# A linear-attention kernel with a gated state space layer: a new order of the opening, and other turns in two steps of its main loop

## The chip, the cores and the metric

One core of a Trainium2 chip runs the whole kernel. The metric is the device time of one execution in microseconds (us). Engines are named as in the profile: PE is TensorE's matrix multiplication and PEld its weight load, DVE is VectorE, ACT is ScalarE, POOL is GpSimd, SP is SyncE, which here only issues transfers.

## The reference

```python
def _attn_ref(q, k, v, alpha):               # each (4, 8, 768, 48)
    state = np.zeros((B, H, D, D))
    for t in range(S):
        state = alpha[:, :, t, :, None] * state + np.einsum('bhd,bhe->bhde', k[:, :, t], v[:, :, t])
        y[:, :, t] = np.einsum('bhd,bhde->bhe', q[:, :, t], state)
    return y

def _moe_ref(x, w_in, A_log, w_out):         # w_in (384, 1024), w_out (512, 384)
    proj = x @ w_in
    val, gate = proj[..., :D_inner], proj[..., D_inner:]
    a = np.exp(A_log)
    for t in range(S):
        h = a * h + val[:, t, :]
        ys[:, t, :] = h
    return (gate / (1 + np.exp(-gate)) * ys) @ w_out

# x is y as (4, 768, 8 * 48)
```

A recurrent attention with a decay for each element and step, in 4 batches of 8 heads, feeds a projection, a scan over time, a gate and a second projection. w_in, A_log and w_out arrive as float64.

## The kernel before, in words

`fast` cuts each batch's 768 steps into 3 groups of 256, 12 groups in all (0 to 11). A group has two chunks of 128 steps (c) and four of 64 (u). Heads 0 to 3 lie in partitions 0 to 63, heads 4 to 7 in 64 to 127 (i is 0 or 1).

**Attention of a group m.** alpha, q and k are turned, so that the steps lie along the free dimension. For groups 0 to 3 (alpha) and 0 to 2 (q, k) TensorE does it: `turned` writes a PSUM bank with 8 or 16 small products against the identity, or by transposes for a few named cases, and `copy_turned` copies it out. From then on VectorE transposes blocks of 32 (`turn`). VectorE runs two scans over a group, `scan_P` forward (running products of alpha, P) and `scan_V` backward (V), and multiplies: Zk is k times V, Zq is q times P. `scores` are products of Zk and Zq into two banks with tags s0, s1 (chunk 0) and two of the four shared banks "mm" (chunk 1). `masks` multiplies by a triangle on VectorE (A) and copies the rest on ACT; from group 3 on, half of the masking is done by POOL on AK. `values` multiplies with v into the banks y, `states` forms the states of the chunks, `add_up` or `add_banks` sums these (sum), `carried` adds what earlier states bring, and `join` copies the result out and moves it by transfers into xT, heads side by side. The main loop calls `first` (scores, masks), `second` (across values, states, sums on POOL) and `third` (carried, values, join).

**State space layer of a group n.** `project(n, cc)` for cc 0 to 3: 6 products of xT with w_in into a pair of "mm" banks, a scan on VectorE (hh), Silu on ACT (sg), a product sg times hh (f). The pairs of banks take turns, so a projection waits until the one before the last has been read by its scan and its Silu. `output(n)` multiplies f with w_out, 8 products of 384 columns, and stores.

**Order.** The schedule is written by hand: each engine runs its instructions in the order of the program's text, and waits for what they need. Step n of the main loop works on layer n and on attention m = n + 1. VectorE's work for groups 4 to 11 is a generator, `products`, of seven pieces (alpha turned, P, k turned, V, Zk, q turned, Zq); `go(count)` runs the next pieces. In steps 3 to 10 a step reads: second(m), go(4), project 0, go(1), project 1, go(1), project 2, go(1), project 3, third(m), first(m+1), output(n). In step 2 the order is first(3), go(1), project 0, second(3), go(2), and so on.

**Weights.** Both weight matrices come as 64-bit words and are made into 32-bit floats: ACT takes the low bits (`low`), VectorE the high ones, POOL adds. w_in is loaded in three units of columns: cc 0, cc 1, cc 2 and 3.

**Opening.** Transfers of alpha, q, k of group 0 go out in two halves, by SP (heads 0 to 3) and by ACT (heads 4 to 7). TensorE warms up on zeros (`keep_warm`), turns alpha, q, k of group 0, then alpha, k of group 1, and so on as attention of group 0 permits; all of q of group 1 is turned between its scores and its values. A small write of POOL into raw_a keeps the second set of loads back.

Of the kernel before, what the change touches and what calls it, by code (L numbers as in the profile page):

```python
# [9 lines left out]
FP32 = mybir.dt.float32  # L10
# [336 lines left out]
def fast(  # L347
# [41 lines left out]
    p2 = pool("p2", 2)  # L389
    ps_at = pool("ps_at", 1, space=PS)  # L390
# [56 lines left out]
    units = [range(0, 1), range(1, 2), range(2, 4)]  # L447
# [45 lines left out]
    def constants():  # L493
# [22 lines left out]
        nc.vector.memset(K0[:, :, :, D:], 0.0)  # L516
# [22 lines left out]
    def low(i):  # L539
        bits, w = bits_of(i)  # L540
        r = p2.tile([C, UW], I32, tag="wr", name="wr")
        lows[i] = r.rearrange("p (a n) -> p a n", a=w.shape[1])
        halves = lows[i].bitcast(U16).rearrange("p a (n two) -> p a n two", two=2)
        nc.scalar.activation(halves[:, :, :, 0], bits[:, :, :, 0], AF.Copy, scale=2.0 ** -29)

    def convert(i):
        if i not in lows:
            low(i)
        bits, w = bits_of(i)
        r = lows.pop(i)  # L550
        halves = r.bitcast(U16).rearrange("p a (n two) -> p a n two", two=2)
        quarters = bits.rearrange("p a n two -> p a (n two)").bitcast(U16).rearrange("p a (n four) -> p a n four", four=4)
        nc.vector.tensor_scalar(out=w.bitcast(U32), in0=bits[:, :, :, 1], scalar1=3, scalar2=0x3FFFFFFF,
                                op0=ALU.logical_shift_left, op1=ALU.bitwise_and)
        nc.vector.tensor_scalar(out=halves[:, :, :, 1], in0=quarters[:, :, :, 3], scalar1=0xC000, scalar2=None,  # L555
                                op0=ALU.bitwise_and)
        nc.gpsimd.tensor_tensor(out=w.bitcast(I32), in0=w.bitcast(I32), in1=r, op=ALU.add)  # L557
# [126 lines left out]
    def turned(m, name, js, t):  # L684
        raw = steps_of(name, m)
        tp = t[:, 0:len(js) * C].rearrange("p (j x) -> p j x", j=len(js))
        if (m, name) in ((1, "k"), (1, "q"), (3, "a")):
            for n, j in enumerate(js):
                nc.tensor.transpose(tp[:, n], raw[:, ds(ROW + j * D - 64, C)], ident)  # L689
                nc.tensor.transpose(tp[0:64, n], raw[:, ds(j * D, 64)], ident)  # L690
            return tp.rearrange("p j (c h) -> p h c j", h=4)
# [6 lines left out]
    def copy_turned(to, js, tp, engine=None):  # L698
        place = by_runs(to)[:, :, :, js.start:js.stop]
        if engine:  # L700
            return engine.tensor_copy(out=place, in_=tp)
        return nc.scalar.activation(place, tp, AF.Copy)

    def turn_over(m, name, to, tags=(None, None)):
        size = NJ // len(tags)
        copies = []
        for n, tag in enumerate(tags):
            js = range(size * n, size * (n + 1))
            copy = copy_turned(to, js, turned(m, name, js, bank(tag)), nc.vector if n % 2 and tag else None)
            if tag:  # L710
                for other in copies[(n + 1) % 2::2]:
# [3 lines left out]
    def alphas(m, tags=(None, None)):  # L715
        turn_over(m, "a", by_place(als[m % 2])[:, :, 1:GP], tags)
# [31 lines left out]
    def masks(m):  # L748
        sc = [[t[:, 0:4 * (L + D)].rearrange("p (h x) -> p h x", h=4) for t in pair] for pair in scs.pop(m)]
        mb = mask[:, None, :]  # L750
        if m < NG:
            for c in range(G):
# [162 lines left out]
    def project(n, cc, late=False):  # L915
# [10 lines left out]
        for vg, kk in order:  # L926
            nc.tensor.matmul((pv, pg)[vg], w_ins[cc][:, kk, vg, :], xT[:, kk, :],  # L927
                             start=(kk == 0), stop=(kk == NK - 1))
# [10 lines left out]
        sg = p2.tile([C, GC], FP32, tag="sg", name="sg")  # L939
# [43 lines left out]
    alphas(0, ("s0", "s1", "y1", "y0"))  # L983
    tq = straighten(0, "q")
    tk = straighten(0, "k")
    alphas(1)
    P = scan_P(0)
    V = scan_V(0, P, False)
    halves = [range(0, NJ // 2), range(NJ // 2, NJ)]
    parts = [turned(1, "k", js, bank()) for js in halves]  # L990
# [3 lines left out]
    scores(0)  # L994
    tk = plain("k")
    for js, part in zip(halves, parts):
        copy_turned(tk, js, part)
    low(0)
    parts = [turned(1, "q", js, bank()) for js in halves]
    convert(0)  # L1000
    nc.gpsimd.memset(raws["a"][0:1, 0:1], 0.0)
    load_steps("a", 2, [nc.sync])
    load_w(units[2], nc.sync)
    masks(0)
    low(1)
    first_values(True)
    st = states(0)
    convert(1)
    first_states(st)
    tq = plain("q")  # L1010
    for js, part in zip(halves, parts):
        copy_turned(tq, js, part)
    last = P[:, :, GC]
    nc.scalar.activation(ratio[:, 0], last, AF.Copy, scale=1.0 / FIRST_PRODUCT)
    nc.scalar.activation(lower[:, :, 0], last, AF.Copy)
    for name in "kqa":
        load_steps(name, 2 + (name == "a"), [nc.sync])
    load_v(1, nc.sync)
# [3 lines left out]
    first_carried((2, 3))  # L1022
    first_join()
    nc.scalar.activation(a_dec, a_log, AF.Exp)
# [25 lines left out]

    for n in range(N):
        m = n + 1
        if n == 0:
            V = scan_V(1, P)
            f0 = project(n, 0)
# [3 lines left out]
            f1 = project(n, 1)  # L1059
# [168 lines left out]
```

## Time and profile before

| | |
|---|---|
| three executions | 279.72 us median, 278.26 to 280.07 |
| the profiled execution | 279.43 us, of which the span from first to last instruction is 277.7 us |
| PE busy | 268.8 us (97%) |
| DVE busy | 218.3 us (79%) |
| POOL busy | 122.4 us (44%) |
| ACT busy | 108.6 us (39%) |
| granted TensorE clock | 1.000 over the span |
| first projection (L927) starts at | 23.39 us |
| last output products start at | 269.30 us |

The timeline gives for each engine the start, the length, the line, the tiles (out<-in) and the number of instructions of a run, and in brackets how long the engine stood idle before it and what ended that. The chain of waits goes back from the last instruction, at each step to what released it. A matmul on 32-bit floats appears as two records, a transpose as one.

### The profile page before, as it was taken

How to read it: one execution, taken by the hardware profiler on the slowest of the kernel's cores; microseconds unless marked ns; L12 is line 12 of the kernel's file. 1: busy time of each engine (PE TensorE's matmuls, PEld its weight loads, DVE VectorE, ACT ScalarE, POOL GpSimd, SP SyncE). 2: the span in 40 equal slices, each digit the busy share in tenths (PEclk: the TensorE clock that was granted, in tenths of full speed). 3: DMA queues.
4: the chain of work that ended last, by engine and by line, in shares of the span. 5: the costliest groups of instructions: out<-in, count | busy, mean ns of one | idle time of the engine just before them, and what ended most of it. 6: DMA issues, size and time to landing. Idle time of an engine off the chain costs nothing.

```text
span 277.7 us, 9598 instructions
## 1 busy us (share of the span) xinstructions
PE 268.8 (97%) x4056; PEld 217.0 (78%) x4056; DVE 218.3 (79%) x281; ACT 108.6 (39%) x244; POOL 122.4 (44%) x141
## 2 busy tenths in 40 slices
PE   7999999999989999899999999999999999999995
PEld 5988887876678688488688688688688688787874
DVE  7979998898798995995895995996995993079540
ACT  2577763461332532341542433433434425213111
POOL 8141223130068574563473584484384476435000
PEclk9999999999999999999999999999999999999999
DMA  6949993845919777487468587576687501201201
GB/s 196 295 140 309 296 262 78 205 88 139 267 48 238 149 199 182 103 214 163 103 181 199 114 205 164 130 197 155 152 186 159 144 0 27 77 1 33 71 5 59
DMA packets 51599, 41.18 MB, mean 148 GB/s; under 512 B 27360, under 2 KB 49536, under 8 KB 51552
## 3 DMA queue, kind: packets, MB, share of 16 engines
q1 hardware_dynamic: 48752, 37.50, 53.1%
q0 software_dynamic: 1408, 2.03, 2.8%
q10 hardware_dynamic: 1392, 0.99, 1.2%
q8 instruction: 33, 0.54, 0.9%
q14 instruction: 14, 0.11, 0.2%
HBM read 32.54 MB, written 4.72 MB: 134 GB/s over the span
## 4 chain that ended last, share of the span: by engine, by line
PE 92%; DVE 3%; DMA 1%; POOL 1%; issue 1%; ACT 1%; SPq 0%; DVEq 0%; ACTq 0%
PE mm L927 45%; PE mm L956 21%; PE y L791 4%; PE y L778 4%; PE mm L744 3%; PE s L744 3%; PE s L810 3%; PE mm L694 2%; PE mm L1189 2%; DMA raw_a<-in_alpha_dram 1%; POOL AK L762 1%; DVE P L630 1%; DVE V L649 1%; PE mm L689 1%; PE y L862 1%
## 5 line engine op out<-in xcount | busy, mean ns | idle before, releaser
L927 PE MATMUL mm<-xT,w_in 128*128 128x256 f32 x576 | 128.9, 382 | 0.6 <-ACT xT L884 0.6
L927 PEld LDWEIGHTS mm<-xT,w_in 128*128 128x128 f32 x576 | 108.1, 190 | 16.3 <-issue 0.8
L956 PE MATMUL mm<-w_out,f_last 128*128 128x384 f32 x160 | 54.1, 492 | 1.3 <-DVE A L759 1.3
L940 ACT ACTIVATE sg<-mm 128x256 f32<-128x256 f32 x48 | 18.4, 384 | 85.8 <-PE mm L927 80.3
L956 PEld LDWEIGHTS mm<-w_out,f_last 128*128 128x128 f32 x160 | 29.7, 190 | 21.1 <-issue 1.4
L830 POOL TENSOR_TENSOR sum<-sum,dS 128x192 f32<-128x192 f32 x30 | 33.2, 1108 | 27.3 <-PE mm L927 13.5
L942 POOL TENSOR_TENSOR f_last<-sg,hh 128x256 f32<-128x256 f32 x36 | 30.9, 862 | 30.6 <-ACT sg L940 23.1
L932 DVE TENSOR_TENSOR_SCAN hh<-a_dec,hh,mm 128x256 f32<-128x256 f32 x32 | 23.4, 732 | 15.4 <-PE mm L927 15.2
L630 DVE TENSOR_TENSOR_SCAN P<-al,lower 128x1028 f32<-128x1028 f32 x12 | 31.1, 2595 | 0.6
L649 DVE TENSOR_TENSOR_SCAN V<-al,ends 128x1028 f32<-128x1028 f32 x12 | 28.3, 2356 | 0.4
L907 POOL DMA_DIRECT2D xT<-yst x40 | 20.5, 517 | 13.1 <-ACT yst L904 11.8
L950 ACT ACTIVATE o_sb<-mm 128x384 f32<-128x384 f32 x22 | 10.8, 491 | 38.4 <-PE mm L956 38.4
L762 POOL TENSOR_TENSOR AK<-AK,mask 128x512 f32<-128x512 f32 x9 | 13.2, 1464 | 17.2 <-ACT AK L760 17.2
L759 DVE TENSOR_TENSOR A<-s,mask 128x256 f32<-128x256 f32 x9 | 3.8, 425 | 21.5 <-PE s L744 21.5
L557 POOL TENSOR_TENSOR w_in<-w_in,wr 128x768 int32<-128x768 int32 x4 | 7.3, 1826 | 26.0 <-DVE wr L555 17.0
L595 DVE STREAM_TRANSPOSE k<-raw_k 128x1024 f32<-128x1024 f32 x9 | 18.3, 2033 | 0.0
L595 DVE STREAM_TRANSPOSE q<-raw_q 128x1024 f32<-128x1024 f32 x9 | 18.2, 2022 | 0.0
L778 PEld LDWEIGHTS y<-AK,v 64*64 64x64 f32 x352 | 12.1, 134 | 6.4 <-issue 5.0
L595 DVE STREAM_TRANSPOSE al<-raw_a 128x1024 f32<-128x1024 f32 x8 | 16.3, 2041 | 0.1
L778 PE MATMUL y<-AK,v 64*64 64x64 f32 x352 | 14.5, 221 | 1.0 <-POOL AK L762 1.0
L791 PEld LDWEIGHTS y<-Zq,sum 48*64 48x64 f32 x656 | 11.8, 134 | 4.3 <-issue 4.1
L791 PE MATMUL y<-Zq,sum 48*64 48x64 f32 x656 | 14.4, 221 | 0.6 <-issue 0.6
(158 smaller groups left out, 392.2 us busy)
## 6 DMA issues: line engine op xcount, KB each, us to landing
v<-in_v_dram SPq DMA_DIRECT2D x22, 192.0 KB, 3.3
out_dram<-o_sb SPq DMA_DIRECT2D x22, 192.0 KB, 2.1
raw_k<-in_k_dram SPq DMA_DIRECT2D x18, 184.0 KB, 3.4
raw_q<-in_q_dram SPq DMA_DIRECT2D x18, 184.0 KB, 3.8
raw_k<-in_k_dram SPq DMA_DIRECT2D x18, 176.0 KB, 3.8
raw_q<-in_q_dram SPq DMA_DIRECT2D x18, 176.0 KB, 4.1
raw_a<-in_alpha_dram SPq DMA_DIRECT2D x16, 184.0 KB, 5.0
raw_a<-in_alpha_dram SPq DMA_DIRECT2D x16, 176.0 KB, 5.1
```

The costliest lines, as they stand in the source:

```text
L595: nc.vector.transpose(out=by_runs(to).rearrange("p h c j -> p h j c"), in_=raws[name][:, 0:4 * ROW].rearrange("p (h j d) -> p h j d", h=4, ...
L630: nc.vector.tensor_tensor_scan(out=P, data0=al[:, 0:4 * GP], data1=lower.rearrange("p h t -> p (h t)"), initial=0.0, op0=ALU.mult, op1=ALU ...
L649: nc.vector.tensor_tensor_scan(out=V[:, ::-1], data0=al[:, 1:4 * GP + 1][:, ::-1], data1=ends.rearrange("p h t -> p (h t)")[:, ::-1], init ...
L778: nc.tensor.matmul(ys[m][i][ds(64 * s, 64), e, ds(c * C + h * L, L)], v_sb[rows, c, 4 * i + p, :], As[i][rows, c, p, :], start=across and ...
L791: nc.tensor.matmul(ys[m][i][ds(64 * s, 64), e, ds(u * L, L)], Ss[j][rows, p, :], Zqs[m % 2][rows, u, p, D:], start=False, stop=True, skip_ ...
L830: nc.gpsimd.tensor_add(Ss[j][:, :, 0:D], Ss[j - 1][:, :, 0:D], part)
L907: engines[n % len(engines)].dma_start(out=xT[to, a], in_=st[rows, i, e])
L927: nc.tensor.matmul((pv, pg)[vg], w_ins[cc][:, kk, vg, :], xT[:, kk, :], start=(kk == 0), stop=(kk == NK - 1))
L932: nc.vector.tensor_tensor_scan(out=hh, data0=a_dec[:, cc:cc + 1].to_broadcast([C, GC]), data1=pv, initial=prev_h[cc][:, GC - 1:GC] if n % ...
L940: nc.scalar.activation(sg, pg, AF.Silu)
L942: f = lambda: engine.tensor_mul(fs[n][cc], sg, hh)
L956: nc.tensor.matmul(os[c], fs[n][cc][:, ds(c * C, C)], w_outs[cc // 2][:, cc % 2, :], start=(cc == 0), stop=(cc == NI - 1))
```

## The change

- `first_alphas` turns alpha of group 0 by products of 64x64, thirty-two in place of sixteen, into the same four banks by quarters, heads 4 to 7 first; ACT copies two banks and VectorE two, as before.
- `first_q` turns q of group 0 with heads 4 to 7 a few products ahead, and the last four of heads 0 to 3 by transposes. k of group 0 and alpha of group 1 are turned by transposes.
- Memsets of dS, of K0 and of the pads of sums leave VectorE; the pads are written by six copies on ACT.
- k and q of group 1 are turned and copied by halves: half of k ahead of the scores, half behind them, half of q then, and the last half behind the carried products of group 0. The masks of group 0 are called by chunks, the first unit's high bits between them. The second unit's bits are taken in two halves ahead of `first_states`.
- The write that keeps the second loads back is made by ACT, later. The upper half of w_in's columns is loaded as two units, the second behind k, q and alpha; its low bits are taken later (`low(3)`).
- In step 0 the third projection is cut in two, with values, states and sums of group 1 between. The products f of the first two projections move to step 1 (sg gets four buffers for that).
- In step 2 `second(3)` moves behind project 1. In step 3 `first(5)` moves behind output(3), and in step 4 `second(5)` moves behind project 1, with go(2) ahead of project 0 and go(2) behind it.

```diff
+    gates = pool("gates", 4)
...
-    units = [range(0, 1), range(1, 2), range(2, 4)]
+    units = [range(i, i + 1) for i in range(NI)]
...
-        for t in dS[0] + dS[1]:
-            nc.vector.memset(t[:, :, :, D:64], 0.0)
-        for t in sums:
-            nc.vector.memset(t[:, :, D:64], 0.0)
-        nc.vector.memset(K0[:, :, :, D:], 0.0)
...
+    turned_by_transpose = ((0, "k"), (1, "a"), (1, "k"), (1, "q"), (3, "a"))
...
+    def first_alphas():
+        raw, to = steps_of("a", 0), by_runs(by_place(als[0])[:, :, 1:GP])
+        tps = [[bank(tag)[:, 0:NJ // 2 * 64].rearrange("p (j x) -> p j x", x=64) for tag in tags]
+               for tags in (("s0", "s1"), ("y1", "y0"))]
+
+        def turn_quarter(j, i, r):
+            rows = ds(64 * r, 64)
+            nc.tensor.matmul(tps[j // 4][r][ds(64 * i, 64), j % 4], raw[rows, ds(i * ROW + j * D, 64)],
+                             ident[rows, rows], start=True, stop=True, skip_group_check=True)
+
+        for j in range(2):
+            for r in range(2):
+                turn_quarter(j, 1, r)
+        for j in range(NJ):
+            for r in range(2):
+                turn_quarter(j, 0, r)
+                if j + 2 < NJ:
+                    turn_quarter(j + 2, 1, 1 - r)
...
     keep_warm(3, 256)
-    alphas(0, ("s0", "s1", "y1", "y0"))
-    tq = straighten(0, "q")
+    first_alphas()
+    for t in sums:
+        nc.scalar.activation(t[:, :, D:64], wide_S[0][:, 0:4 * (64 - D)].rearrange("p (j d) -> p j d", j=4), AF.Copy)
+    tq = first_q()
     tk = straighten(0, "k")
     alphas(1)
     P = scan_P(0)
...
-    parts = [turned(1, "k", js, bank()) for js in halves]
+    part = turned(1, "k", halves[0], bank())
     for c in range(G):
         scaled_k(0, tk, V, c)
         scaled_q(0, tq, P, c)
...
+    copy_turned(tk, halves[0], part)
+    for c in range(G):
+        scores(0, (c,))
+    part = turned(1, "k", halves[1], bank())
+    masks(0, (0,))
     low(0)
+    high(0)
+    masks(0, (1,))
+    add_low(0)
+    copy_turned(tk, halves[1], part)
+    part = turned(1, "q", halves[0], bank())
+    first_values(True)
+    st = states(0)
+    for vg in range(2):
+        low(1, slice(vg, None, 2))
+        high(1, slice(vg, None, 2))
+    first_states(st)
+    add_low(1)
+    copy_turned(tq, halves[0], part)
+    nc.scalar.activation(raws["a"][0:1, 0:1], wide_S[1][0:1, D:D + 1], AF.Copy)
     load_steps("a", 2, [nc.sync])
     load_w(units[2], nc.sync)
...
+    load_w(units[3], nc.sync)
     load_v(1, nc.sync)
     P = scan_P(1)
     first_carried((1,))
     first_values(False)
     first_carried((2, 3))
+    part = turned(1, "q", halves[1], bank(), False)
     first_join()
+    copy_turned(tq, halves[1], part)
...
+    late = (1, 3)
...
-            f2 = project(n, 2)
-            values(m, True)
-            st = states(m)
-            add_banks(m, st)
+            f2 = project(n, 2, between=across_and_states)
...
+            for f in fs_late:
+                f()
...
-                go(1)
-                f0 = project(n, 0)
-                second(m)
-                go(2)
-            else:
+            if n - 1 not in late:
                 second(m)
                 go(4)
-                f0 = project(n, 0)
+            else:
+                go(n // 2)
+            f0 = project(n, 0)
             f0()
+            if n - 1 in late:
+                go(2)
             load_raw("k", n + 3, nc.sync)
             load_raw("a", n + 3, nc.sync)
             go(1)
             f1 = project(n, 1)
             f1()
+            if n - 1 in late:
+                second(m)
...
             third(m)
-            first(m + 1)
+            if n not in late:
+                first(m + 1)
...
         if 0 < n < N - 1:
             output(n)
+        if n > 1 and n in late:
+            first(m + 1)
```

More of the change, by code (lines that the diff above doesn't have):

```diff
@@ L548, in convert @@
             low(i)
[L549 to L557, printed above, removed]
+        high(i)
+        add_low(i)
     def check_w(i):
@@ L696, in turned @@
         return tp.rearrange("p j (c h) -> p h c j", h=4)
[L698 to L705, printed above, removed]
-        copies = []
[L707 to L711, printed above, removed]
+    halves = [range(0, NJ // 2), range(NJ // 2, NJ)]
@@ L913, in fast, with project @@
     fs = {}
-    def project(n, cc, late=False):
+    def project(n, cc, late=False, between=None):
         if cc == 0:
```

112 lines of the change are left out of this document (71 added, 41 removed).

## The prediction

> **What bounds the kernel now.** I read the page first, then the timeline of TensorE for its idle time, then the chain of waits stage by stage. The page says whose kernel this is:
>
> ```profile
> PE 268.8 (97%) x4056; PEld 217.0 (78%) x4056; DVE 218.3 (79%) x281; ACT 108.6 (39%) x244; POOL 122.4 (44%) x141
> ```
>
> TensorE is busy 97% of the span. The change adds and removes hardly any matrix work, so it can win only what TensorE waits for, or what runs slowly in the opening. The large waits, from TensorE's timeline (start, length, instruction, and in brackets the idle time before it and what ended it):
>
> ```profile
> 23.39 5.42 PE L927 MATMUL mm<-xT,w_in 128*128 128x256 f32 x24 [0.56 <-ACT xT L884]
> 44.15 0.35 PE L791 MATMUL y<-Zq,sum 48*64 48x64 f32 x9 [0.65 <-issue]
> 78.97 0.27 PE L778 MATMUL y<-AK,v 64*64 64x64 f32 x2 [1.01 <-POOL AK L762]
> 112.81 0.56 PE L956 MATMUL mm<-w_out,f_last 128*128 128x384 f32 x1 [1.25 <-DVE A L759]
> ```
>
> Behind 23.39 us three waits of 0.65, 1.01 and 1.25 us are nearly all there is: 2.9 us, 1.04% of the span. Ahead of 23.39 VectorE's scans lead, and there the chain shows what an earlier start would move (start, length, what; x counts records, two to a matmul):
>
> ```profile
> 4.79 1.56 PE s L694 x16
> 6.35 0.91 PE y L694 x16
> 7.29 0.47 DVE al L701
> ...
> 7.87 2.31 DVE P L630
> ...
> 15.47 1.00 PE mm L744 x32
> ...
> 18.43 0.90 PE y L862 x40
> ...
> 19.90 0.34 ACT wide_S L877
> 20.24 0.04 issue
> 20.28 0.62 PE y L870 x22
> ...
> 22.88 0.37 ACT xT L884
> ```
>
> **Part one: the opening, -0.5 us.** The sixteen half turns of alpha become thirty-two quarter turns of 64x64. A 64x64 matmul costs 0.47/32 us a record in the row at 88.74 further down, so 64 records take about 0.95 us at full speed, against 1.82 for the 32 wide ones at the pace of the row at 6.35. But the first part of it runs slowly in any case: the sixteen records at 4.79 took 1.56 us where the next sixteen took 0.91. So the first copies start about where they do now (6.0), and what is saved is in the second pair: ACT and VectorE copy side by side (0.47 each), 6.0 to 6.5 and 6.5 to 7.0, and the scan P of group 0 starts at 7.1 in place of 7.87. That VectorE is free at 6.0 is the memsets' doing, which held it to 6.45 (6.28 + 0.17); their six replacements on ACT delay only q's copies, and q is first used behind two scans. I take 0.77 us for this step (0.3 if the quarters pack no better than the row at 18.43, 0.90/40 a record; 1.0 at best).
>
> VectorE's chain is then 0.77 earlier to its second Zq, and the second scores start at 14.7 in place of 15.47. Behind them stand half of k's turns and half of q's, 0.9 us each, in place of all of q's (1.8). The price of a turn does not move by transposing:
>
> ```profile
> L694 PE MATMUL mm<-ident,raw_k 128*64 128x128 f32 x32 | 1.9, 272 | 0.0
> L689 PE MATMUL mm<-ident,raw_k 128*128 128x128 f32 x8 | 1.9, 279 | 0.0
> ```
>
> 32 records of the one, or 8 of L689 with 8 of L690 between them, fill 1.9 us alike; k and the alphas of group 1 by transposes cost nothing and bring nothing. The values then start at 14.7 + 1.0 + 1.8 = 17.5 in place of 18.4; VectorE's last mask, 17.62 in the row below, comes to about 16.9 and is in time. Here something else is late: the bits of the second weight unit.
>
> ```profile
> 6.28 0.17 DVE L516 MEMSET K<- 128x128 f32 x1
> 17.20 0.42 DVE L754 TENSOR_TENSOR AK<-mm,mask 128x256 f32<-128x256 f32 x1
> 18.50 1.10 ACT L544 ACTIVATE wr<-wbits 128x768 uint16<-128x768 uint32 x1 [0.51 <-DMA wbits<-in_moe_w_in_dram]
> 28.57 1.08 ACT L544 ACTIVATE wr<-wbits 128x768 uint16<-128x768 uint32 x1 [1.23 <-DMA wbits<-in_moe_w_in_dram]
> ```
>
> ACT waited for that transfer to 18.5. Its issue is not moved, so neither is its landing. In the new order ACT takes the low bits in two halves (0.55 each) ahead of the first state's copy: the half that landed first is done before 18.5, the other from 18.5 to 19.05, and the copy of wide_S starts at 19.05, not at 17.5 + 19.90 - 18.43 = 18.9. That is 0.85 earlier than 19.90. From there to the end of the carried products are 22.88 - 20.28 = 2.6 us, so 19.43 + 2.6 = 22.0; then the other half of q's turns (0.9), under which ACT's copy of xT (0.37) hides, and the first projection starts at 22.9 in place of 23.39: -0.5. It is less than the 0.77 put in because 0.9 us of turning now stands where TensorE idled 0.56. Bounds: -1.0 when the late half of the bits does not hold ACT, +0.3 when the quarters bring nothing and the transfer comes half a microsecond later.
>
> The upper weight columns as two units: the first is half as long, the second queues behind k, q and alpha on SP, 0.8 us after the old start. Its low bits are now taken behind q's copies of group 2, well after the row at 28.57, where ACT's wait for the whole old transfer ended: nothing.
>
> **Part two: group 0's late products and the split third projection, -0.2 us.** Two multiplications leave VectorE ahead of the scan of group 2, so Zk and Zq of that group come earlier.
>
> ```profile
> 33.13 0.75 DVE L942 TENSOR_TENSOR wide<-sg,hh 128x256 f32<-128x256 f32 x2
> ```
>
> TensorE did not wait for them. The 0.65 at 44.15 has no releaser in the profile; values and states move ahead of half a projection there. I count a third of it, bounds 0 and -0.65.
>
> **Part three: turns in step 2, -0.5 us.** The across products of group 3 go behind two projections, not one. Rows of the chain, then of VectorE's and GpSimd's timelines:
>
> ```profile
> 80.38 7.97 PE mm L927 x36
> ...
> 88.74 0.47 PE y L778 x32
> ```
>
> ```profile
> 83.23 2.21 POOL L830 TENSOR_TENSOR sum<-sum,dS 128x192 f32<-128x192 f32 x2
> 84.23 0.73 DVE L932 TENSOR_TENSOR_SCAN hh<-a_dec,hh,mm 128x256 f32<-128x256 f32 x1
> 98.58 0.60 POOL L830 TENSOR_TENSOR sum<-sum,dS 128x192 f32<-128x192 f32 x1 [4.08 <-ACT dS L818]
> 99.35 4.14 POOL L830 TENSOR_TENSOR sum<-sum,dS 128x192 f32<-128x192 f32 x2 [0.18 <-POOL sum L830]
> ```
>
> The first projection ended at 78.97 - 1.01 = 77.96, values and states took 80.38 - 78.97 = 1.41. With a second projection (7.97/3 = 2.65) ahead of them the wait of 1.01 is gone. What is late next: the fourth projection wants the banks of the second, which the scan hh at 84.23 frees at 84.96; TensorE comes there at 77.96 + 2.65 + 1.41 + 2.65 = 84.67, so 0.3 is given back. And the three sums on POOL now stand behind the second gate product, which waits for that same scan: from 85.7 on they need 1.8 us (0.60 each) to 3.3 (1.1 each), the last by about 88.7. So -0.7 to +0.5; I take -0.5.
>
> **Part four: turns in steps 3 and 4, +1.8 us.** The scores of group 5 go behind output(3), 5.4 us later. VectorE runs in program order, and its masks stand ahead of all its work for group 6:
>
> ```profile
> 109.32 0.70 PE y L791 x48
> ...
> 119.54 10.56 PE mm L927 x48
> ...
> 131.65 0.77 PE s L744 x32
> ```
>
> ```profile
> 110.84 0.42 DVE L759 TENSOR_TENSOR A<-s,mask 128x256 f32<-128x256 f32 x1 [2.95 <-PE s L744]
> 111.61 0.42 DVE L759 TENSOR_TENSOR A<-mm,mask 128x256 f32<-128x256 f32 x1 [0.34 <-PE mm L744]
> ...
> 114.29 2.74 DVE L630 TENSOR_TENSOR_SCAN P<-al,lower 128x1028 f32<-128x1028 f32 x1
> ...
> 123.73 0.75 DVE L932 TENSOR_TENSOR_SCAN hh<-a_dec,hh,mm 128x256 f32<-128x256 f32 x1
> ...
> 126.98 1.20 DVE L605 TENSOR_TENSOR Zq<-q,P 128x1024 f32<-128x1024 f32 x1
> ```
>
> TensorE: group 4's last attention product ends at 110.02, output(3) takes 5.36 to 115.4 without the wait of 1.25 (it no longer stands behind those scores), the scores twice 0.77 to 116.9, two projections 5.28 to 122.2, group 5's values and states 119.54 - 118.2 = 1.3 to 123.5, the third projection to 126.2. VectorE: the second mask ended 0.47 behind the scores, now 117.35. From there to the end of the second hh its rows need 124.48 - 112.03 = 12.45, less 0.43 if P runs at the 2.31 of the row at 7.87: about 129.3. The fourth projection waits for that hh's banks, 126.2 to 129.3: **a new wait of 3.1 us**. Then 2.65 and the attention products (1.56, as from 130.1 to 131.65): scores of group 6 at 133.5, and Zq of group 6 (126.98 + 1.20 - 112.03 = 16.15 behind the mask) is ready at 133.1 to 133.5. Against 131.65 this is 1.85 late; I take 1.8. VectorE idled 2.95 us ahead of these masks already; now it idles 8, and that is where the price comes from. Bounds: 0.5, if VectorE runs its 16 us a microsecond faster; 3.3, by the POOL sums below.
>
> [...]
>
> **The sum.** -0.5 - 0.2 - 0.5 + 1.8 = +0.6. The profiled execution took 279.43 us (span 277.7 and 1.7 around it), 0.3 under the median of 279.72 and within its 278.26 to 280.07. **Forecast: 280.0 us**, no change that a measurement of this kernel (about 1%, 2.8 us) can tell.
>
> **Rivals.**
> (a) *The turns are free*: VectorE catches up, and parts three and four bring their whole 1.01 + 1.25. With the opening 279.43 - 0.5 - 0.2 - 2.26 = 276.5. For it: VectorE idles about 3 us ahead of every pair of masks. Against: its row shows 16.15 us of work where TensorE has 13.5. Chance 0.10.
> (b) *The opening brings nothing*, because bits or loads land later: 279.43 + 0.3 - 0.2 - 0.5 + 1.8 = 280.8. Chance 0.15.
> (c) *The sums on POOL decide step 4* (slower). They stand behind the second gate product, so behind the hh that ends at 129.3: with 1.5 for the product and 4.14/2 for each sum the last comes at 137.0, the scores of group 6 at 137.3, 3.8 later than above: 283.8. It decides once the sums end after 133.2. For it: 4.14 at 99.35; against: 0.60 at 98.58, between VectorE's scans, and what VectorE runs from 129.3 on is a transpose. Chance 0.08.
> (d) *The clock drops in the opening* (slower). q's turns end near 8.4 (alpha 6.4, then 2.0, since four of them have no partner); then transposes of k (1.8), alpha (1.8) and k (0.9) fill TensorE to 12.9 with no other product between.
>
> ```profile
> 1.44 2.93 PE L726 MATMUL y<-wide_S 128*128 128x256 f32 x6 [1.44 <-DVE raw_q L498]
> ```
>
> Six records took 2.93 us at the start, 0.43 apart where 48 of that width take 10.56, 0.22 apart: half speed. If the turns left TensorE there again until about 16, its 2.9 us of half turns and scores would double: 279.4 + 0.6 + 2.9 = 282.9. Against it: the eight pairs on raw_k ran at 0.11 a record in the row of L689 with scores right behind, and nothing slowed. Chance 0.07. [...]
>
> The forecast itself has 0.60. **Range** 277.9 to 283.0: (a) and the upper part of (c) are left out. Faster by over 1%: half of (a) and a little of the forecast's tail, 0.07. Slower by over 1%: (c), half of (d) and a tail, 0.13. Within 1%: 0.80.
>
> **What would show it.** First projection near 22.9; P of group 0 near 7.1; no wait for POOL AK at 79; none at output(3); a wait of about 3 us of L927 on DVE hh in step 4, and VectorE idle some 8 us ahead of the masks of group 5. I am wrong if that wait is under 1 us or if the opening moves by over 1 us.

## The result and the profile after

The changed kernel takes 280.62 us in the median of 22 executions (278.77 to 282.11), the kernel before beside it 279.2 us (278.26 to 280.09, also 22). The ratio is 1.0048, 95% interval 1.0029 to 1.0067: half a percent slower, resolved by so many executions but within the 1% that the prediction calls no change. The forecast was 280.0.

The profiled execution took 280.11 us, with a span of 278.4 (before: 279.43 and 277.7). The head of the page, and the waits of TensorE grouped by line (us in total, times, longest):

```profile
PE 269.9 (97%) x4060; PEld 216.6 (78%) x4060; DVE 215.9 (78%) x272; ACT 109.9 (39%) x252; POOL 119.2 (43%) x140
...
PE mm L974 <- DVE hh L981: 2.2, 1, 2.2
PE y L772 <- DVE raw_q L499: 1.4, 1, 1.4
PE y L916 <- ACT wide_S L923: 0.5, 1, 0.5
PE y L837 <- issue: 0.5, 1, 0.5
```

The waits of 1.01 us for POOL AK and of 1.25 us at output(3) are gone, and one wait of 2.2 us has come. Where it stands, from TensorE's timeline (L1008 is the output's line, L790 the scores', L974 the projections'):

```profile
109.20 5.43 PE L1008 MATMUL mm<-w_out,f_last 128*128 128x384 f32 x16
114.56 1.00 PE L790 MATMUL s<-Zq,Zk 48*64 48x112 f32 x32
...
122.96 2.86 PE L974 MATMUL mm<-xT,w_in 128*128 128x256 f32 x12
128.04 2.86 PE L974 MATMUL mm<-xT,w_in 128*128 128x256 f32 x12 [2.23 <-DVE hh L981]
```

The first projection ends part one; behind each later part the two kernels have a place in common, the first scores of a group. From the chains of waits, first the kernel before, then the changed one:

```profile
73.47 0.93 PE s L744 x32
...
89.67 0.77 PE s L744 x32
...
110.02 0.77 PE s L744 x32
```

```profile
73.50 0.93 PE s L790 x32
...
88.69 1.00 PE s L790 x32
...
109.27 5.36 PE mm L1008 x16
...
132.46 0.77 PE s L790 x32
```

| up to | before | after | difference | this part | forecast |
|---|---|---|---|---|---|
| first projection | 23.39 | 23.62 | +0.23 | opening +0.2 | -0.5 |
| scores of group 3 | 73.47 | 73.50 | +0.03 | part two -0.2 | -0.2 |
| scores of group 4 | 89.67 | 88.69 | -0.98 | part three -1.0 | -0.5 |
| scores of group 6 | 131.65 | 132.46 | +0.81 | part four +1.8 | +1.8 |
| span | 277.7 | 278.4 | +0.7 | | +0.6 |

The trace is 0.7 us longer, but the medians are 1.4 apart. The rest is the clock. The granted clock is the share of full speed at which TensorE was allowed to run. Of the 22 executions, 11 show a mean granted clock of 0.999 or 1.000, like the profiled one, and have a median of 279.75 us; the other 11 show 0.993 or 0.994, and theirs is 281.4. Of the kernel before, no execution timed beside the experiments was under 0.998. A second profile of the changed kernel (below) fell on the lower clock and shows where it is lost.

### The profile page after: what moved, and what is told of

It is laid out like the page before. It is cut to its first block, busy times and chain, and to the rows that moved or that the text cites. A ratio compares the mean times of both kernels' runs of the same rounds, so it can differ in the third digit from the quotient of the medians.

```text
span 278.4 us, 9643 instructions
## 1 busy us (share of the span) xinstructions
PE 269.9 (97%) x4060; PEld 216.6 (78%) x4060; DVE 215.9 (78%) x272; ACT 109.9 (39%) x252; POOL 119.2 (43%) x140
## 4 chain that ended last, share of the span: by engine, by line
PE 87%; DMA 5%; DVE 3%; issue 2%; SPq 1%; ACT 1%; DVEq 0%
PE mm L974 43%; PE mm L1008 21%; PE y L837 4%; PE y L824 4%; PE s L790 3%; PE mm L790 3%; DMA wbits<-in_moe_w_in_dram 3%; PE s L856 3%; PE mm L700 2%; PE mm L1256 2%; DMA raw_q<-in_q_dram 2%; DVE V L653 1%; DVE al L599 1%; DVE k L599 1%; SPq L422 1%
## 5 line engine op out<-in xcount | busy, mean ns | idle before, releaser
L974 PE MATMUL mm<-xT,w_in 128*128 128x256 f32 x576 | 129.7, 382 | 2.2 <-DVE hh L981 2.2
L974 PEld LDWEIGHTS mm<-xT,w_in 128*128 128x128 f32 x576 | 107.9, 190 | 18.4 <-DVE hh L981 2.6
L1008 PE MATMUL mm<-w_out,f_last 128*128 128x384 f32 x160 | 54.2, 492 | 0.0
L994 POOL TENSOR_TENSOR f_last<-sg,hh 128x256 f32<-128x256 f32 x36 | 33.1, 922 | 40.0 <-DVE hh L981 23.2
L1008 PEld LDWEIGHTS mm<-w_out,f_last 128*128 128x128 f32 x160 | 29.7, 190 | 19.8
L876 POOL TENSOR_TENSOR sum<-sum,dS 128x192 f32<-128x192 f32 x30 | 29.4, 980 | 21.4 <-ACT dS L864 11.8
L634 DVE TENSOR_TENSOR_SCAN P<-al,lower 128x1028 f32<-128x1028 f32 x12 | 31.9, 2655 | 0.5
L609 DVE TENSOR_TENSOR Zq<-q,P 128x1024 f32<-128x1024 f32 (+1 forms) x14 | 15.0, 1072 | 0.0
L618 DVE TENSOR_TENSOR Zk<-k,V 128x1024 f32<-128x1024 f32 (+1 forms) x14 | 14.7, 1053 | 0.1
```

What stands on the lines that cost most here:

```text
L634: nc.vector.tensor_tensor_scan(out=P, data0=al[:, 0:4 * GP], data1=lower.rearrange("p h t -> p (h t)"), initial=0.0, op0=ALU.mult, op1=ALU ...
L876: nc.gpsimd.tensor_add(Ss[j][:, :, 0:D], Ss[j - 1][:, :, 0:D], part)
L994: f = lambda: engine.tensor_mul(fs[n][cc], sg, hh)
L1008: nc.tensor.matmul(os[c], fs[n][cc][:, ds(c * C, C)], w_outs[cc // 2][:, cc % 2, :], start=(cc == 0), stop=(cc == NI - 1))
```

## Experiments

**1. The turns of steps 3 and 4 put back.** The opening and step 2 stay as in the change.

```
-    late = (1, 3)
+    late = (1,)
```

> The changed kernel with the turns of steps 3 and 4 put back (scores of group 5 ahead of output(3), values and states of group 5 at the start of step 4); step 2 and the opening stay changed. In the changed kernel's trace the stretch from the end of group 4's attention products to the scores of group 6 grew from 21.63 to 23.19 us. Theory (VectorE's lateness is the price): the wait of 2.23 us ahead of the fourth projection of step 4 is gone, VectorE stands idle about 3 us ahead of the masks of group 5, not 7.9, and the time falls by about 1.6 us, to 279.0. Rival (the order of output and scores was what made the wait of 1.25 us before): that wait comes back, and the stretch is 21.6 us as it was. Rival (the wait was no matter of the order): it stays away, and the stretch is about 20.4. On the clock: 11 of the 22 executions of the changed kernel show a granted clock of 0.993 or 0.994 and take 281.4 us in the median, the others 0.999 or 1.000 and 279.75. If TensorE's idle 2.23 us in step 4 lets the clock drop, every execution here shows 0.999 or more, and the time falls by 0.7 us more.

Measured: 278.56 us, ratio 0.9991 (0.9968 to 1.0013), 2.1 under the changed kernel. The clock did not follow the expectation: four of the twelve executions are at 0.994. From TensorE's timeline:

```profile
108.80 0.93 PE L790 MATMUL mm<-Zq,Zk 48*64 48x112 f32 x28
111.05 0.41 PE L790 MATMUL mm<-Zq,Zk 48*64 48x112 f32 x4 [1.31 <-issue]
111.39 5.43 PE L1008 MATMUL mm<-w_out,f_last 128*128 128x384 f32 x16
118.08 10.63 PE L974 MATMUL mm<-xT,w_in 128*128 128x256 f32 x48
```

The wait in step 4 is gone: the four projections run through. The wait of 1.25 us has come back at a place a little earlier: TensorE stands still for 1.31 us in the middle of the scores, where no engine holds it. VectorE's mask, to which the profile of before puts that wait down, does not hold the output: here output(3) starts at 111.39 and the second mask only at 111.49. The wait does go with the order: in the four profiles with these scores ahead of output(3) (before, experiments 1, 7 and 8) TensorE stands still for 0.86 to 1.68 us there, and in the eight with the scores behind it not at all. More on such gaps below.

**2. Alpha of group 1 and k of group 0 turned by products again.** Only the way of turning in the opening is undone.

```
-    turned_by_transpose = ((0, "k"), (1, "a"), (1, "k"), (1, "q"), (3, "a"))
+    turned_by_transpose = ((1, "k"), (1, "q"), (3, "a"))
```

> The changed kernel with k of group 0 and alpha of group 1 turned by products again, not by transposes; all else stays changed. Theory (clock): a stretch of 4.4 us in which TensorE runs transposes alone, at about 8 to 12.5 us, makes the clock drop in half of the executions; with products there the granted clock is 0.999 or more in all, and the median falls by about 0.7 us to 279.9. Rival (the clock drops for another reason, for example the idle time in step 4): half of the executions still show 0.993 or 0.994, and the median stays at 280.6. The price of a turn itself is the same both ways, 1.75 us for sixteen, so the profile's first projection stays at 23.6.

Measured: 283.2 us, ratio 1.011 (1.0074 to 1.0146). Slower, not faster, and of the six executions three are at 0.994 and one, of 288.13 us, at 0.988: with these transposes gone the clock drops all the same. The slowness is not all clock, since the two executions at full clock take 281.68 and 281.33 us. In the profile TensorE stands still twice with no releaser, longer than in either profile of the changed kernel: in the carried products and, at 197.90, ahead of an output. The first row is from the timeline; the second is the page's for the products with w_out (busy us, mean ns, idle us before them and what ended most of it). Whether the other executions have these gaps isn't known.

```profile
22.65 0.45 PE L916 MATMUL y<-Zq,wide_S 48*64 48x64 f32 x7 [0.93 <-issue]
```

```profile
L1008 PE MATMUL mm<-w_out,f_last 128*128 128x384 f32 x160 | 54.1, 492 | 1.7 <-issue 1.7
```

**3. The low bits of the second weight unit behind the first state's copies.**

```
+    first_states(st)
     for vg in range(2):
         low(1, slice(vg, None, 2))
         high(1, slice(vg, None, 2))
-    first_states(st)
```

> The changed kernel with one move: the copy and the sums of the first states come ahead of the low and high bits of the second weight unit on ACT and VectorE, not behind them. Theory (the transfer of those bits eats the opening's gain: ACT waits to 18.20 us, works on the bits to 19.2, and only then copies wide_S): wide_S is copied at about 18.5 in place of 19.19, the carried products start at 18.9 in place of 19.55, and the first projection at 22.8 in place of 23.62; the time falls by about 0.8 us. Rival (TensorE's own work, or the supply of its instructions, sets the first projection): it stays within 0.3 us of 23.62, and a gap with no releaser stands in the carried products.

Measured: 281.94 us, ratio 1.0095 (1.0072 to 1.0118), all six executions at 0.994 or less. ACT's and TensorE's timelines:

```profile
18.90 0.33 ACT L923 ACTIVATE wide_S<-s 128x192 f32<-128x192 f32 x1 [1.27 <-PE s L856]
21.25 0.39 PE L916 MATMUL y<-Zq,wide_S 48*64 48x64 f32 x7 [1.50 <-issue]
24.52 0.70 PE L974 MATMUL mm<-xT,w_in 128*128 128x256 f32 x2
```

The copy of wide_S is 0.3 us earlier than in the changed kernel (19.19), no more, since now TensorE's states end last. What that gives is lost again, with more, in the carried products, which stand still for 1.50 us with no releaser. Part of the longer time is the clock: the changed kernel's executions at the lower clock have 281.4.

**4. The turns alone, on the kernel before.** The opening of before, late = (1, 3) and the turns of steps 2 to 4 of the change.

> The kernel before with the new turns of steps 2, 3 and 4 alone (values and states of group 3 and of group 5 behind project 1, scores of group 5 behind output(3)); opening, step 0 and step 1 as before. Theory (what the traces of before and after show): the wait of 1.01 us at 79 is gone, the one of 1.25 at output(3) too, a wait of 2.2 us ahead of the fourth projection of step 4 comes; the sum over steps 2 to 4 is +0.6 to +0.8 us, time 279.9. If the idle time in step 4 is what lets the clock drop, about half of the executions here show a granted clock of 0.993 or 0.994 as well, and the median is about 280.6; if the opening's transposes do it, all show 0.999 or more.

Measured: 281.65 us, ratio 1.0089 (1.0059 to 1.0119); five of six executions at 0.994 or less, with a median of 281.68. That is 0.3 over the changed kernel at the lower clock, so by this comparison the new opening and steps 0 and 1 bring 0.3 us. The wait is there without any of the new opening:

```profile
127.81 4.54 PE L927 MATMUL mm<-xT,w_in 128*128 128x256 f32 x12 [2.46 <-DVE hh L932]
```

Twelve records take 4.54 us here, where they take 2.86 in the changed kernel's profile: behind the wait they run at half speed (granted clock 0.50 from 127.94 to 131.35).

**5. The changed kernel again**, for another profile.

> The changed kernel once more, for a second profiled execution. In the first, TensorE ran dry for 0.27 us at 20.28 and 0.49 us at 44.16 with no releaser, each about 2.5 us behind the start of a packet of its instruction queue; in the kernel with the bits later such a gap of 1.50 us stood at 21.25, 2.6 us behind such a packet, with the same instructions on TensorE. If the place of these refills belongs to the program, the packets start at 12.8, 17.6 and 21.4 us here too and the gaps are as before. If it belongs to the execution, they move by a microsecond or more and so do the gaps. On the clock: if the wait of 2.23 us in step 4 lies whole in one window of the clock (windows of 3.41 us, counted from the rise of the clock near 5 us), the half clock follows and the time is about 281.4; if it is cut by a window's end, it does not, and the time is about 279.8.

Measured: 280.89 us, clock 0.994. The instruction packets are not where they were: those that started at 12.77, 17.57 and 21.44 us start at 8.44, 17.13 and 20.77. No gap of 0.27 us stands in the carried products, the one of 0.49 at 44.16 is 0.23 at 43.26, and the first projection starts at 22.98 in place of 23.62. So these gaps belong to the execution, not to the program alone.

For the clock, two tables by stretches of time (its us, busy time of each engine, then the granted clock, the share of the DMA engines, GB/s), this execution first, then the first profile of the changed kernel:

```profile
124.47:127.89 3.42, 1.19 (x6) 0.72 (x5) 3.42 (x6) 0.38 (x1) 0.66 (x1) 1.00 0.89 220
127.89:131.31 3.42, 3.42 (x10) 2.69 (x8) 3.42 (x4) 0.00 (x0) 3.26 (x5) 0.50 1.07 240
131.31:134.72 3.41, 3.41 (x163) 2.96 (x161) 0.72 (x2) 1.75 (x5) 1.44 (x3) 1.00 0.74 155
```

```profile
124.27:127.68 3.41, 1.55 (x8) 1.01 (x6) 3.41 (x5) 0.38 (x1) 0.00 (x0) 1.00 0.75 195
127.68:131.09 3.41, 3.04 (x28) 2.46 (x32) 3.41 (x4) 0.00 (x0) 2.80 (x5) 1.00 1.05 226
```

The clock was released at 5.01 us, fell at 127.89 and rose at 131.31, one stretch of 3.413 us at 0.50. From the release to the fall are 122.88 us, 36 times 3.413; it is the same 122.88 in the second, third and fourth experiment, which also fall right at this wait (at 129.05, 128.42 and 127.94). In the profiles of the kernel before and of the changed kernel, both at full clock, it falls only at the end of the program, 273.07 us behind the release, which is 80 times 3.413. So every change of the clock read here lies a whole number of windows of 3.413 us behind its release, and the fall follows a window with 1.19 us of TensorE's work in it (1.25, 1.18 and 0.95 in the second, third and fourth experiment). In the first profile the window border cut the same wait otherwise, 1.55 us of work stood in the window, and the clock stayed. That the little work in one window makes the clock fall is a reading of these five profiles; that 2.23 us of idle time in it (3.42 less 1.19) can be enough is what they show. A window at half clock costs about 1.7 us (half of 3.413); the medians of the two kinds of execution differ by 1.65. One such window in 279 us makes a mean of 0.994.

**6. Two pieces of group 6 ahead of the late scores.** In the changed kernel VectorE is idle ahead of the masks of group 5 and has too much to do behind them. This takes alpha's transpose and the scan P of group 6 into the idle stretch:

```
-            else:
-                go(n // 2)
+            elif n == 2:
+                go(1)
...
         if n > 1 and n in late:
+            go(2)
             first(m + 1)
```

> The changed kernel with VectorE's first two pieces for group 6 (alpha's transpose and the scan P) ahead of the late scores and masks of group 5, in the time in which VectorE stands idle, in place of behind them; TensorE's order is that of the changed kernel. Theory (VectorE's lateness behind the masks is the price of the turns in steps 3 and 4): VectorE's work from those masks to Zq of group 6 falls from 14.8 to about 10.5 us, the wait of 2.23 us at 128 is gone, no execution shows the half clock for it, and the time falls by 1.6 us for the wait and by 0.7 for the clock, to about 278.4. Rival (the banks or GpSimd's sums are late next): a wait of over 1 us stays ahead of the third or fourth projection of step 4, or ahead of the carried products, and the time stays above 279.5.

Measured: 276.87 us in five executions, ratio 0.9907 (0.9883 to 0.9931), clock 0.998 or more throughout: faster than both kernels, and 1.5 us under the 278.4 expected. From the scores of group 4 to those of group 6 the profile has 41.28 us, where the changed kernel's has 43.77: 2.5 less, not 1.6. A sixth execution took 706.64 us and is left out; what it was isn't settled, and it did not come again (last experiment).

**7. All turns of the main loop as before.** The opening and steps 0 and 1 stay.

```
-    late = (1, 3)
+    late = ()
...
-            if n - 1 not in late:
+                go(1)
+                f0 = project(n, 0)
                 second(m)
-                go(4)
-            else:
-                go(n // 2)
-            f0 = project(n, 0)
+                go(2)
+            else:
+                second(m)
+                go(4)
+                f0 = project(n, 0)
```

> The changed kernel with all three turns of the main loop put back (steps 2 to 4 as before); what is left of the change is the opening and steps 0 and 1. The two traces put the scores of group 2 at 44.54 us before and 44.56 after, so by them the opening brings nothing: 279.2, within 0.3 us of the kernel before, with the waits of about 1.0 at 79 and, where the refill of instructions falls as before, 1.25 at 112. Rival (what the prediction said, -0.7 us for these parts): 278.5. Rival (the opening is worse in most executions, because it runs TensorE dry of instructions where the first profile showed only 0.27 us): 280 or more. The clock is 0.999 or more in all executions if the wait in step 4 is what lets it drop.

Measured: 278.52 us, ratio 0.9989 (0.997 to 1.0009), all at 0.998 or more.

```profile
77.71 0.27 PE L824 MATMUL y<-AK,v 64*64 64x64 f32 x2 [1.01 <-POOL AK L808]
...
111.14 0.41 PE L790 MATMUL mm<-Zq,Zk 48*64 48x112 f32 x5 [0.86 <-issue]
```

The wait for AK is back to the hundredth, and the one at output(3) stands in the middle of the scores again, 0.86 us long. The median is that of the first rival, 278.5 (279.5 for the kernel before beside it), but the ratio's interval reaches from 0.8 us less to 0.3 us more: it doesn't tell the -0.7 of the prediction from nothing.

**8. Bits later without the turns of steps 3 and 4** (the edits of the third and first experiments together).

> The bits of the second weight unit behind the first states, as in the earlier experiment, on the kernel that has the turns of steps 3 and 4 put back. That kernel took 278.56 us with the first projection at 23.31 us. Theory (the transfer holds the opening up): wide_S is copied before the bits land, and where no refill of instructions falls into the carried products the first projection comes at about 22.6 and the time is about 277.8. Rival (TensorE runs dry of instructions once the rest is early): a gap of over 1 us with no releaser stands in the carried products again, the first projection is at 23.5 or later, and the time 278.8 or more.

Measured: 279.63 us, ratio 1.0034 (1.0008 to 1.006); 1.07 us over the same kernel with the bits where the change puts them. Neither the theory nor the rival describes the profile: the first projection comes at 22.95, 0.3 us earlier than in the first experiment, with a gap of no more than 0.25 us in the carried products, but the scores of group 3 start at 73.14 where the first experiment has 72.44. So what is gained ahead of the first projection is lost, with more, behind it.

**9. One piece ahead.** A dose between the changed kernel and the sixth experiment.

```
             else:
-                go(n // 2)
+                go(1)
...
         if n > 1 and n in late:
+            go(1)
             first(m + 1)
```

> The changed kernel with one of the two pieces moved: VectorE transposes alpha of group 6 (2.05 us) ahead of the scores of group 5, in place of behind their masks; the scan P of that group stays behind the masks. A dose between the changed kernel and the one with both pieces moved. Theory (the price is VectorE's row behind the late masks, and the half clock follows the length of the wait): the wait ahead of the fourth projection of step 4 falls from 2.23 us to 0.1 to 0.3; with so little idle time no stretch at half clock follows, in any execution; the time is 280.6 less 2.05 less half of 1.65 = 277.7. Rival 1 (VectorE's row is not what holds the fourth projection): the wait stays near 2.2 and the time near 280.6. Rival 2 (the half clock has nothing to do with this wait): granted clocks of 0.994 in about half of the executions go on, and the median is 280.6 less 2.05 = 278.6, with a spread as wide as that of the changed kernel.

Measured: 277.54 us, ratio 0.9948 (0.9924 to 0.9971), all ten executions at 0.998 or more. Its waits hold the row

```profile
PE mm L974 <- DVE hh L981: 0.3, 1, 0.3
```

in place of 2.2: nearly the 2.05 us of the transpose, taken off the wait (2.23 to 0.27), and no half clock behind what is left. Both parts of the price follow the dose.

**10. Both pieces once more**, the kernel of the sixth experiment.

> The kernel with both pieces (alpha's transpose and the scan P of group 6) ahead of the late scores once more, for the size of its gain over the kernel before and for the one long execution of 706 us. Theory: 276.9 us within 0.5, 0.9% under the kernel before, the interval wholly under 0.995, granted clock at least 0.998 in every execution. Rival (the lead was luck of one chip or of where the instruction packets fell): 278 or more, the interval reaches 0.997. For the long execution: if it belongs to this kernel it comes again in about one of six; if it was a single event, none of these shows it.

Measured: 276.96 us (276.17 to 277.42), ratio 0.9928 (0.9909 to 0.9946), no clock under 0.998 and no long execution in six. Of TensorE's waits by line only the one at the very start is left in the profile, and VectorE's timeline shows the two pieces in the stretch that was idle:

```profile
PE y L772 <- DVE raw_q L499: 1.4, 1, 1.4
```

```profile
106.62 2.05 DVE L599 STREAM_TRANSPOSE al<-raw_a 128x1024 f32<-128x1024 f32 x1
108.61 0.06 DVE L633 MEMSET lower<- 128x4 f32 x1
108.71 2.30 DVE L634 TENSOR_TENSOR_SCAN P<-al,lower 128x1028 f32<-128x1028 f32 x1
114.62 0.42 DVE L805 TENSOR_TENSOR A<-s,mask 128x256 f32<-128x256 f32 x1 [3.62 <-PE s L790]
```

## Why the prediction was right, and where it wasn't

The forecast of 280.0 and its sum of +0.6 against a trace of +0.7 agree better than their terms, and that is luck: in this pair of profiles the opening was 0.7 us too good, step 2 0.5 too poor, and what the clock adds to the median was not in it.

**Part one, the opening, failed: +0.2 in place of -0.5.** The turning itself gave what was forecast. P of group 0 starts at 6.55, not 7.1, but part of that is the clock, which is released at 4.80 us here and at 5.78 in the profile of before. Where the releases are alike, P starts 0.9 us earlier than with the old opening (6.97 against 7.87, released at 5.76 in the seventh experiment and at 5.78 before) or 0.8 (6.65 against 7.45, released at 5.01 in the fifth and 5.06 in the fourth); 0.77 was forecast. In this profile VectorE's chain is 1.3 us ahead, and still nothing is left of it at 23.6. The step that failed is "the half that landed first is done before 18.5". ACT's and VectorE's timelines:

```profile
17.08 0.59 ACT L707 ACTIVATE k<-mm 128x512 f32<-128x512 f32 x1
18.20 1.13 ACT L542 ACTIVATE wr<-wbits 128x384 uint16<-128x384 uint32 x2 [0.53 <-DMA wbits<-in_moe_w_in_dram]
...
19.19 0.30 ACT L923 ACTIVATE wide_S<-s 128x192 f32<-128x192 f32 x1
```

```profile
16.39 0.42 DVE L800 TENSOR_TENSOR AK<-mm,mask 128x256 f32<-128x256 f32 x1
18.20 0.43 DVE L548 TENSOR_SCALAR w_in<-wbits 128x384 uint32<-128x384 uint32 x1 [1.38 <-DMA wbits<-in_moe_w_in_dram]
```

Both halves wait for the later transfer, though the first had landed at 17.14, and both run from 18.20 on; VectorE, free from 16.81, idles 1.38 us for the same landing. That the copy still came at 19.19 and not at 19.5 is only because the transfer landed 0.3 earlier than in the trace of before. The other 0.6 are sizes: the carried products took 3.05 us (19.55 to 22.60) against 2.6, 0.27 of it standing still, and the last turns of q 1.02 against 0.9:

```profile
9.84 8.33 DMA wbits<-in_moe_w_in_dram
...
19.55 0.46 PE y L916 x16
20.01 0.27 issue
20.28 0.39 PE y L916 x6
...
22.60 1.02 PE mm L700 x16
23.62 5.38 PE mm L974 x24
```

One pair of profiles does not give the size of this, since the landing differs from execution to execution. These are the profiles with the old opening and with the new one as the change has it (times in us):

| profile | ACT and VectorE take up the second unit's bits at | from there to the first projection | from the first projection to the scores of group 3 |
|---|---|---|---|
| before | 18.50 | 4.89 | 50.08 |
| experiment 4, old opening | 18.15 | 4.89 | 49.98 |
| changed kernel | 18.20 | 5.42 | 49.88 |
| the same, experiment 5 | 18.06 | 4.92 | 49.61 |
| experiment 1 | 18.31 | 5.00 | 49.13 |
| experiment 6 | 19.34 | 4.93 | 49.59 |
| experiment 7 | 17.71 | 5.18 | 49.33 |
| experiment 9 | 18.63 | 5.18 | 49.12 |
| experiment 10 | 18.19 | 5.21 | 49.12 |

In all nine both engines start right behind the landing of the later transfer. The prediction reckoned 4.4 us from there to the first projection (18.5 to 22.9); the new opening takes 4.9 to 5.4, no less than the old one's 4.9. So the landing sets the first projection in both, and VectorE's lead is waited away. Where the bits are taken later (experiments 3 and 8), the copy of wide_S comes only 0.3 us earlier than in the changed kernel, or 0.6: TensorE's states end next. The first projection itself comes between 22.89 and 24.27 with the new opening: the +0.2 is one of a spread.

Rival (b), that the opening brings nothing, holds at the first projection, though not through a later landing: in the first profile the transfer came 0.3 us earlier and was waited for whole.

**Part two** hit -0.2 in the first profile, by luck; the 0.65 at 44.15 is 0.49 at 44.16. In the table's other six profiles with the new opening the stretch from the first projection to the scores of group 3 is 0.4 to 1.0 us shorter than with the old opening, which goes beyond the bound of -0.65, and that gap is 0.23 and 0.20 us in experiments 5 and 6 and under 0.15 in the others. Parts one and two together were forecast at -0.7. By the scores of group 3, which start at 72.22 to 73.86 us with the new opening (72.59 in the middle) and at 73.47 and 73.02 with the old, that is near. By the whole time they bring about 0.3 us in the fourth and seventh experiments, and the seventh's interval holds both 0 and 0.7.

**Part three** was right in kind, and its gain doubled, by the same 1.0 us in every profile that has the turn of step 2: the wait of 1.01 is gone whole, the 0.3 said to be given back at the second hh did not come (the third and fourth projections run through), and the three sums on POOL came in time.

**Part four** was right at +1.8, with a smaller wait than forecast, 2.23 in place of 3.1. VectorE's timeline, the row of work named in the prediction:

```profile
115.61 0.42 DVE L805 TENSOR_TENSOR A<-s,mask 128x256 f32<-128x256 f32 x1 [7.93 <-PE s L790]
116.37 0.42 DVE L805 TENSOR_TENSOR A<-mm,mask 128x256 f32<-128x256 f32 x1 [0.34 <-PE mm L790]
116.71 2.05 DVE L599 STREAM_TRANSPOSE al<-raw_a 128x1024 f32<-128x1024 f32 x1
...
127.25 0.74 DVE L981 TENSOR_TENSOR_SCAN hh<-a_dec,hh,mm 128x256 f32<-128x256 f32 x1
```

It idled 7.93 us (forecast 8), and needed 11.2 us from the second mask to the end of hh (116.79 to 127.99) where 12.0 were reckoned, because small rows ran shorter and two idles of 0.15 were gone. The smaller wait with the same +1.8 means that something else took longer: 2.23 less the 1.25 at output(3) is 0.98, and the first halves of the scores of groups 4 and 5 take 1.00 and 0.93 us in the chain where they took 0.77; the rest is spread over small steps and the restart behind the wait (twelve records in 2.86 us, where a quarter of the 10.56 of before is 2.64). The step that named the old order as the cause of the 1.25 is borne out by the twelve profiles, though the profile's name for it, VectorE's mask, is not (first experiment).

**The clock was the missing term**, about +0.8 in the median (half of the executions by 1.65). Rival (d) had the half speed, but at the wrong place: in the four profiles that caught it (experiments 2 to 5) it came behind the idle time in step 4, not in the transposes of the opening. In the changed kernel's profile the stretch of transposes alone ran at full clock:

```profile
8.21:12.56 4.35, 4.35 (x43) 4.33 (x40) 4.18 (x5) 3.26 (x6) 0.00 (x0) 1.00 0.99 293
```

That a stretch of transposes lowers the clock was a guess, and no run shows it. Rival (c) did not come. The three sums on GpSimd:

```profile
128.82 1.97 POOL L876 TENSOR_TENSOR sum<-sum,dS 128x192 f32<-128x192 f32 x3
```

That is 0.66 us each, far from 4.14/2. Rival (a) comes near what is to be had once VectorE's idle time is filled: it reckoned 2.9 us under the kernel before, and the last experiment has 2.1 (276.96 against 279.05).

What stays open: four of twelve executions of the first experiment and five of twelve of the eighth are at 0.994 though the profiles of these kernels have no wait in step 4. Their profiles fell on full clock, so the place wasn't seen, and some of the changed kernel's lower clocks may come from there too. A gap of the kind told in the last section, longer than the 1.31 and 1.68 us of these two profiles, would be a candidate; no run shows one. Why the first half of the bits waits for both transfers isn't shown either.

## What to carry to other kernels

When work is moved later on the engine that leads, look at what stands behind it in program order on the engine that answers, and move as much of that work ahead of it as its idle time holds: here the whole change cost 0.5% as made and gained 0.7 to 0.9% with two pieces moved along. Price an idle stretch of TensorE at its length and at what the clocks of many executions show behind it: here one of 2.23 us cost, in part of the executions, 3.41 us at half clock as well. Before a wait is put down to the engine that the profile names, see in several profiles where it stands. And before an opening is judged by its first projection, look at a second profile of the same kernel: here the two lie 0.64 us apart.

## What was not expected of the hardware

TensorE stands still now and then with nothing in the profile that holds it ("issue"): in the profiles here fourteen times for 0.2 us and over, 1.71 at most, the 1.25 of before counted with them. For nine (two before, two in the changed kernel, one each in experiments 1, 2, 3, 7 and 8) the start of a packet of DMA queue q8 is known, which the page lists as instructions (33 of 16 KB): these gaps end 2.3 to 2.8 us behind it. The page's row of this queue in the changed kernel, then the same row for 109.7 to 110.3 us of the kernel before and for 18.5 to 19.0 us of the third experiment:

```profile
q8 instruction: 33, 0.54, 0.9%
```

```profile
q8 instruction: 1, 0.02, 12.1%
```

```profile
q8 instruction: 1, 0.02, 14.8%
```

The gaps behind them end at 112.81 (1.25 us) and 21.25 (1.50 us). All of them lie in stretches of many small matmuls: scores, carried and attention products, or right behind one (1.71 us ahead of an output of the second experiment). That is how a gap that the profile of before puts down to VectorE's mask can stand in the middle of the scores elsewhere, put down to nothing (1.31, 0.86 and 1.68 us in the first, seventh and eighth experiments), and be gone where output(3), with its few wide products, stands there instead. Reading it as late instructions fits all of these, but no run took the packets away, so it is argued and not shown.
